# One cosine table folded out of the sine's turns, and small vector work given to GpSimd, in a fused state-space and feed-forward kernel

## The chip, the cores and the metric

The kernel runs on one core of a Trainium2 chip. The core has five engines that each work through their own list of instructions in the written order: TensorE (PE in the profile; its weight loads are PEld), VectorE (DVE), ScalarE (ACT), GpSimd (POOL) and SyncE (SP), which here only issues transfers. An engine that waits for another holds up everything written behind that instruction on its own list. The metric is device microseconds of one execution; the kernel's time is the median over several executions.

## The reference

Two branches read the same normalized input and are added to it. x has 2048 rows (time steps) of 512 features in bfloat16; P = 512 states, F = 1376.

```python
xn = layernorm(x)
# branch A: a diagonal complex state-space model
Lam, Bmat, Cmat = Lambda_re + 1j*Lambda_im, B_re + 1j*B_im, C_re + 1j*C_im
Lam_bar = exp(exp(log_dt) * Lam)
B_bar = ((Lam_bar - 1) / Lam)[:, None] * Bmat
Bu = einsum("bld,pd->blp", xn, B_bar)
for t in range(L):                      # 2048 steps, P complex states
    h = Lam_bar * h + Bu[:, t]
y = 2 * real(einsum("blp,dp->bld", h, Cmat)) + xn * Dskip
# branch B: a gated feed-forward net
f = (silu(xn @ w_gate) * (xn @ w_up)) @ w_down
out = x + y + f
```

## The kernel before, in words

**Tiling.** The 2048 rows are cut into four chunks of 512, and each chunk into four tiles of 128 rows. Tensors are held with features or states on the 128 partitions: 512 features or states are four blocks (NQ = 4), and F = 1376 is ten blocks of 128 and a rest of 96. One matmul takes a 128x128 weight block against 512 columns. All matmul results go to PSUM, which is held as eight banks of 128x512 in float32 (`bank()`); a bank is used again only when the engine that reads its old contents is through.

**What a chunk goes through.** Normalization (`ln_stats` L204, `ln_rstd` L212, `ln_nb` L216; chunks 2 and 3 are normalized on ScalarE by `norm_act` L233 to L236, which needs `nb`), and a transposing transfer on SyncE's queue (`xT_dma`). The projection to the states (`bproj_tile`, matmuls L380, eight groups of four for the real and imaginary part of four blocks; ScalarE copies each bank out at L382). The gate and up products (`gu_mm`, L500; ScalarE evicts gate through Silu at L519 and up at L520; VectorE multiplies the two at L515). The remaining 96 columns of F go through `gateup_last` and `up_pair` (copies to `ul` on ScalarE at L548). The down product (L795 in `out_ffn`, L771 in `out_pair`).

**The complex recurrence made real.** The rotating part of the state is taken off before the recurrence and put back behind it. Tables of cosine and sine of j times the angle (`c16`, `s16`, 128 x 4 x 512 in bfloat16) multiply the projected input; then VectorE runs a real first-order scan per block and part with the modulus `r_t` (L466, eight scans a chunk), and the result is rotated back. A rotation has two forms. `rotation` (L384) does six passes of 128x2048 on VectorE. `rotation_dma` (L414) does four: two `side` products (L423 or L425), two `main` products (L428), and the additions are made by accumulating transfers that GpSimd issues (`join`, L431). It needs the negated sine for one of its sides: `neg_s16`, which `negate_table` (L409) makes on ScalarE in the space of two tiles, `part_end` and `jidx`. Between two chunks the last state is turned by the angle of 512 steps: `carry` (L470 to L482), six operations on 128x4 numbers; the scans of the next chunk start from it.

**The tables** (`table_ops`, L297). For each half of the blocks: `turns` (two products of the index j by the angle in turns), `half` for the sine and again for the cosine (add a quarter turn for the cosine, round by adding a large constant, L314, subtract both, L315), and the two sine activations (L319). Their scratch tiles are named `pm`, of which there are three.

**The coefficients** (`params_b`, L337): sixteen operations on 128x4 numbers that give `c2re`, `nc2re` and `nc2im`, among them a reciprocal. `c_ops` (L354) uses them to fold the input factor into C: ScalarE scales a block of C (L363, tile `cm`), VectorE combines it with the other part (L366, tile `CF`), eight times.

**Outputs.** For chunk 3 the states' output product is eight matmuls a tile (`out_ssm`, L807). For chunks 0, 1 and 2 it is a two-by-two block scheme with seven products in place of eight (`out_ssm_seven`, L670, matmuls L690). Its sums of states and of weights are made by ScalarE and by accumulating transfers (`state_sums`, `weight_sums`), and its results are put together by VectorE (`add`, L702) from PSUM banks and scratch (`six`, `seven`, `one`, `five`, and `finish`, L711, for the four result tiles `res`).

**What sets the order.** The program is written in the order of TensorE's work. VectorE's queue work and the work that goes with it is kept in a list, `backlog`, of operations with a cost in microseconds each (`queue`, L829). After each group of matmuls the program calls `pump` (L845) with the time that the group takes on TensorE. That time is added to `owed`, and operations are taken from the list and written out as long as `owed` is at least half the cost of the first one; each takes its cost off `owed` (`step`, L836). Products and the adds of `out_ssm_seven` also take their cost off. `need(tag)` writes out everything up to the last operation of a tag. `step` also writes out the ScalarE part of the next operations ahead of time (`AHEAD`, for the scalings of L363). So a cost figure decides nothing on the chip, but it decides where in each engine's list an operation stands. The list in question begins with the tables and the normalization of chunk 1 (L954 to L960), goes on with the coefficients and the rotation of chunk 0 (L1073) mixed with the normalization of chunks 2 and 3 (L1075 to L1078), then chunk 1, the folding of C (L1105), chunk 2 (L1115), and chunk 3 (L1131 to L1134).

Of the kernel before, what the change touches and what calls it, by code (L numbers as in the profile page):

```python
# [23 lines left out]
def kernel(  # L24
# [143 lines left out]
    jidx = const.tile([128, CW], F32, name="jidx")  # L168
    nc.gpsimd.iota(out=jidx[:], pattern=[[1, CW]], base=0, channel_multiplier=0, allow_small_or_imprecise_dtypes=True)
# [6 lines left out]
    part_end = const.tile([128, D], F32, name="part_end")  # L176
# [119 lines left out]

    def table_ops():  # L297

        ops = []
        for q0 in range(0, NQ, 2):  # L300
            box = {}

            def turns(q0=q0, box=box):
                box["tt"] = ssm.tile([128, 2, CW], F32, name="pm", bufs=3)
                for qq in range(2):
                    V.tensor_scalar(out=box["tt"][:, qq, :], in0=jidx[:], scalar1=ws2[:, 0, q0 + qq:q0 + qq + 1],
                                    scalar2=None, op0=ALU.mult)

            def half(dst, shift, q0=q0, box=box):
                tt = flat(box["tt"][:])  # L310
                if shift:
                    V.tensor_scalar(out=tt, in0=tt, scalar1=shift, scalar2=None, op0=ALU.add)
                km = box[shift] = ssm.tile([128, 2, CW], F32, name="pm", bufs=3)
# [4 lines left out]
            def sine(dst, shift, q0=q0, box=box):  # L318
                nc.scalar.activation(out=flat(dst[:, q0:q0 + 2, :]), in_=flat(box[shift][:]), func=ACT.Sin,  # L319
                                     scale=-TWO_PI_LO)  # L320

            ops += [(0.9, turns), (1.8, lambda half=half: half(s16, 0.0)),
                    (1.2, lambda half=half: half(c16, 0.25)), (0.6, lambda sine=sine: sine(s16, 0.0)),
                    (0.6, lambda sine=sine: sine(c16, 0.25))]
# [12 lines left out]
    def params_b():  # L337
        tt(t_a[:], lre, lre, ALU.mult)
        tt(t_b[:], lim, lim, ALU.mult)
        tt(den[:], t_a[:], t_b[:], ALU.add)  # L340
        V.reciprocal(out=den[:], in_=den[:])
        tt(lbi[:], r_t[:], sin1[:, 0, :], ALU.mult)
        tt(lbr[:], r_t[:], cos1[:, 0, :], ALU.mult)
        V.tensor_scalar(out=lbr[:], in0=lbr[:], scalar1=-1.0, scalar2=None, op0=ALU.add)
        tt(t_a[:], lbr[:], lre, ALU.mult)
        tt(t_b[:], lbi[:], lim, ALU.mult)
        tt(num_re[:], t_a[:], t_b[:], ALU.add)
        tt(t_a[:], lbi[:], lre, ALU.mult)
        tt(t_b[:], lbr[:], lim, ALU.mult)
        tt(num_im[:], t_a[:], t_b[:], ALU.subtract)  # L350
        for dst, num, s in ((c2re, num_re, 2.0), (nc2re, num_re, -2.0), (nc2im, num_im, -2.0)):
            V.scalar_tensor_tensor(out=dst[:], in0=num[:], scalar=s, in1=den[:], op0=ALU.mult, op1=ALU.mult)
# [54 lines left out]
    neg_s16 = [t[:].bitcast(BF16).rearrange("p (q j) -> p q j", q=2) for t in (part_end, jidx)]  # L407

    def negate_table():  # L409
        for q in range(NQ):  # L410
            yield 1, lambda q=q: nc.scalar.activation(out=neg_s16[q // 2][:, q % 2], in_=s16[:, q], func=ACT.Copy,
                                                      scale=-1.0)

    def rotation_dma(src, dst, back):  # L414
# [3 lines left out]
        def side(i):  # L418
            t = box[i] = ssm.tile([128, NQ, CW], BF16, name="pm", bufs=3)
            if i == (1 if back else 0):  # L420
                for h, table in enumerate(neg_s16):
                    q = slice(2 * h, 2 * h + 2)
                    V.tensor_tensor(out=t[:, q], in0=src()[:, i, q], in1=table, op=ALU.mult)  # L423
            else:
                V.tensor_tensor(out=t[:], in0=src()[:, i], in1=s16[:], op=ALU.mult)  # L425
# [742 lines left out]
```

## Time and profile before

| what | value |
|---|---|
| median of three runs (lowest to highest) | 176.67 us (176.61 to 177.15) |
| the profiled execution | 176.73 us, its span 174.9 us |
| granted TensorE clock, mean | 1.00 |
| TensorE busy | 171.3 us, 98% of the span |
| VectorE busy | 160.2 us, 92% |
| ScalarE busy | 102.6 us, 59% |
| GpSimd busy | 55.1 us, 32% |

The span is the time from the first to the last instruction that the profiler recorded; the execution's own time is 1.8 us longer. In the rows below a line of a timeline has the start, the length, the engine, the line of the kernel, the operation, the tiles it writes and reads, and how many instructions in a row it stands for; square brackets give the idle time before it and what ended it. A line of a group has the count, the busy time, the mean of one in nanoseconds and the idle time before.

### The profile page before, as it was taken

The page shows a single profiled execution, that of the slowest core. Times are in us where ns is not written, and L with a number is a line of the kernel's source. Part 1 is how long each engine was busy: PE and PEld are TensorE (multiplying, and loading weights), DVE is VectorE, ACT ScalarE, POOL GpSimd, SP SyncE. Part 2 cuts the span into 40 slices and gives each one's busy share as a digit, 9 for nine tenths or more (in the row PEclk, how much of TensorE's full clock was granted, in tenths as well). Part 3 has the DMA queues.
Part 4 walks back from the last instruction along what each step waited for, and adds up shares of the span by engine and source line. Part 5 has one row for each costly group of instructions (what it writes and reads, how often), then busy time and mean ns, then how long its engine had stood idle before and what let it go on. Part 6 is the DMA issues. An engine that isn't in the chain of part 4 may idle for free.

```text
span 174.9 us, 2876 instructions
## 1 busy us (share of the span) xinstructions
PE 171.3 (98%) x1026; PEld 90.3 (52%) x1026; DVE 160.2 (92%) x255; ACT 102.6 (59%) x194; POOL 55.1 (32%) x57
## 2 busy tenths in 40 slices
PE   8999999999999999999999999999999999999993
PEld 3877544444444444444444584468444444447743
DVE  3879998999999999899999989997999999995884
ACT  4587898969599889999767760001297632001100
POOL 7050120000300163403555052550473402518440
PEclk9999999999999999999999999999999999999999
DMA  5998499996239079996999988592199999687954
GB/s 161 301 196 198 91 255 91 322 282 139 46 61 287 0 150 168 205 182 175 124 117 128 198 145 100 69 141 43 24 172 207 198 152 237 82 95 78 181 146 139
DMA packets 45758, 26.61 MB, mean 152 GB/s; under 512 B 22272, under 2 KB 44544, under 8 KB 45728
## 3 DMA queue, kind: packets, MB, share of 16 engines
q0 software_dynamic: 12624, 11.67, 47.2%
q1 hardware_dynamic: 30672, 13.61, 34.2%
q10 hardware_dynamic: 2448, 1.15, 2.9%
q8 instruction: 8, 0.13, 0.3%
q14 instruction: 6, 0.05, 0.1%
HBM read 8.33 MB, written 4.19 MB: 72 GB/s over the span
## 4 chain that ended last, share of the span: by engine, by line
PE 96%; DMA 1%; DVE 1%; ACT 0%; issue 0%
PE ps L500 36%; PE ps L380 16%; PE ps L690 11%; PE ps L795 10%; PE ps L771 10%; PE ps L807 4%; PE ps L896 2%; PE ps L553 2%; PE ps L977 2%; PE ps L598 2%; DMA xall<-in_A_x_dram 1%; PE ps L545 1%; PE ps L245 1%; DVE stats L205 0%; ACT gu_last L226 0%; DVE xall L222 0%
## 5 line engine op out<-in xcount | busy, mean ns | idle before, releaser
L500 PE MATMUL ps<-xnT,wu 128*128 128x512 bf16 (+1 forms) x148 | 36.6, 373 | 0.0
L500 PE MATMUL ps<-xnT,wg 128*128 128x512 bf16 (+1 forms) x148 | 36.6, 373 | 0.0
L466 DVE TENSOR_TENSOR_SCAN g<-r_t,car,u 128x512 bf16<-128x512 f32 x24 | 28.8, 1263 | 0.0
L380 PE MATMUL ps<-xnT,BT 128*128 128x512 bf16 x128 | 28.3, 379 | 0.0
L519 ACT ACTIVATE guT<-ps 128x512 bf16<-128x512 f32 (+1 forms) x40 | 24.0, 601 | 5.8 <-PE ps L500 2.8
L520 ACT CAST u_all<-ps 128x512 bf16<-128x512 f32 (+1 forms) x40 | 23.4, 584 | 4.1 <-PE ps L500 4.0
L500 PEld LDWEIGHTS <-wu 128*128 128x128 bf16 x148 | 14.5, 98 | 16.6
L500 PEld LDWEIGHTS <-wg 128*128 128x128 bf16 x148 | 14.4, 98 | 16.5
L382 ACT CAST u<-ps 128x512 bf16<-128x512 f32 x32 | 18.3, 587 | 5.2 <-PE ps L380 5.0
L380 PEld LDWEIGHTS <-BT 128*128 128x128 bf16 x128 | 12.3, 98 | 15.2 <-issue 1.0
L723 ACT COPY guT<-ps 128x512 f32<-128x512 f32 x2 | 1.2, 586 | 28.5 <-PE ps L690 28.5
L795 PE MATMUL ps<-wd_sb,guT 128*128 128x512 bf16 x80 | 17.6, 379 | 0.0
L771 PE MATMUL ps<-wd_sb,guT 128*128 128x512 bf16 x80 | 17.4, 379 | 0.0
L214 POOL TENSOR_TENSOR rstd<-ve,neg_half 128x2 f32<-128x2 f32 (+1 forms) x4 | 5.6, 1390 | 29.9 <-DVE ve L213 29.9
L515 DVE TENSOR_TENSOR guT<-guT,u_all 128x1024 bf16<-128x1024 bf16 x20 | 13.3, 678 | 0.0
L795 PEld LDWEIGHTS <-guT 128*128 128x128 bf16 x80 | 7.7, 98 | 9.6 <-issue 0.4
L771 PEld LDWEIGHTS <-guT 128*128 128x128 bf16 x80 | 7.8, 98 | 9.4
L431 POOL DMA_DIRECT2D wt<-pm x4 | 3.6, 909 | 25.9 <-DVE wt L428 16.7
L205 DVE BATCH_NORM_STATS2 stats<-xall 128x6 f32<-128x512 bf16 x14 | 9.5, 679 | 2.1 <-DMA xall<-in_A_x_dram 2.1
L466 DVE TENSOR_TENSOR_SCAN g<-r_t,u 128x512 bf16<-128x512 f32 x8 | 9.3, 1205 | 0.0
L617 POOL DMA_DIRECT2D xnT<-wt x3 | 3.9, 1290 | 14.0 <-DMA CT<-CF 8.4
L719 POOL DMA_DIRECT2D out_dram<-res x8 | 8.0, 1836 | 0.0
(176 smaller groups left out, 283.9 us busy)
## 6 DMA issues: line engine op xcount, KB each, us to landing
wt<-pm POOLq DMA_DIRECT2D x4, 512.0 KB, 5.0
u<-pm POOLq DMA_DIRECT2D x4, 512.0 KB, 5.9
wd_sb<-in_B_w_down_dram SPq DMA_DIRECT2D x2, 640.0 KB, 8.4
xall<-in_A_x_dram SPq DMA_DIRECT2D x1, 1024.0 KB, 6.5
out_dram<-res POOLq DMA_DIRECT2D x8, 128.0 KB, 5.7
out_dram<-xall POOLq DMA_DIRECT2D x2, 512.0 KB, 8.9
xnT<-wt POOLq DMA_DIRECT2D x3, 256.0 KB, 4.8
xnT<-wt SPq DMA_DIRECT2D x3, 256.0 KB, 7.5
```

What stands on the lines that cost most here:

```text
L205: nc.vector.bn_stats(out=stats[:, n, :], in_=xall[:, n, :])
L380: nc.tensor.matmul(ps[:], lhsT=BT[:, part, k, q * 128:(q + 1) * 128], rhs=xnT[:, k, c * CW:(c + 1) * CW], start=(k == 0), stop=(k == KD - 1))
L382: nc.scalar.copy(out=u_tiles[c][:, part, q, :], in_=ps[:])
L466: V.tensor_tensor_scan(out=g()[:, part, q, :], data0=r_t[:, q:q + 1].to_broadcast([128, CW]), data1=u_tiles[c][:, part, q, :], initial=ini ...
L500: nc.tensor.matmul(ps[:fs, lo:hi], lhsT=wslice(groups, fi, k), rhs=xnT[:, k, c * CW + lo:c * CW + hi], start=(k == 0), stop=(k == KD - 1))
L515: products.append(lambda: V.tensor_tensor(out=g, in0=g, in1=u, op=ALU.mult))
L519: nc.scalar.activation(out=gu_tile(c)[:, fi, 0:hi], in_=psg[:, 0:hi], func=ACT.Silu)
L520: nc.scalar.copy(out=u_tile(c, fi)[:, fi % 2, 0:hi], in_=psu[:, 0:hi])
L690: nc.tensor.matmul(place(i), lhsT=a[:, q, i * 128:(i + 1) * 128], rhs=b[:, q, :], start=(start and q == 0), stop=(stop and q == NQ - 1))
L719: nc.gpsimd.dma_start(out=out_v[:, n, :], in_=res[:], accum_op=ALU.add)
L771: nc.tensor.matmul(o[:], lhsT=gu_tiles[k][:, fi, i * 128:(i + 1) * 128], rhs=wd_sb[:, fi, :], start=(fi == 0), stop=False)
L795: nc.tensor.matmul(o[:], lhsT=gu_tiles[c][:, fi, i * 128:(i + 1) * 128], rhs=wd_sb[:, fi, lo:hi], start=(fi == 0), stop=False)
```

## The change

The cosine table is no longer rounded for itself. `fold` takes the sine's turns, which lie between minus a half and a half, and clears their sign bit (one pass, `bitwise_and` with 0x7fffffff on the bits). The cosine is then the sine of a quarter turn minus that: the second activation has the bias `quarter`, a constant of half of pi that GpSimd writes once. The shift by a quarter turn, the rounding and the subtraction of the cosine go.

`part_end` and `jidx` become two halves of one tile, `ends`, and `neg_s16` is one table over both, so that each negated side is one product and not two.

`params_b` is written for GpSimd, seventeen operations there; only the reciprocal stays on VectorE. The factors of 2 and -2 are now put into `den` between the last products. The six operations of each `carry` are made by GpSimd.

Three cost figures are changed with this: the cosine's rounding at 1.2 becomes `fold` at 0.6, `params_b` goes from 1.5 to 0.1, and `carry` from 0.8 to 0.0. The list and the calls of `pump` stay as they were. VectorE's list therefore lacks what is taken off it and holds the rest of the same work, in places in another order, as the planner writes it out; ScalarE's, GpSimd's and SyncE's lists are in places in another order too. TensorE's list is the same in the same order.

```diff
-    jidx = const.tile([128, CW], F32, name="jidx")
-    nc.gpsimd.iota(out=jidx[:], pattern=[[1, CW]], base=0, channel_multiplier=0, ...)
+    ends = const.tile([128, 2, CW], F32, name="ends")
+    part_end, jidx = ends[:, 0, :], ends[:, 1, :]
+    nc.gpsimd.iota(out=jidx, pattern=[[1, CW]], base=0, channel_multiplier=0, ...)
...
-    part_end = const.tile([128, D], F32, name="part_end")
...
+    quarter = sm("quarter", 1)
+    nc.gpsimd.memset(quarter[:], PI_LO / 2)
...
-            def half(dst, shift, q0=q0, box=box):
+            def half(q0=q0, box=box):
                 tt = flat(box["tt"][:])
-                if shift:
-                    V.tensor_scalar(out=tt, in0=tt, scalar1=shift, scalar2=None, op0=ALU.add)
-                km = box[shift] = ssm.tile([128, 2, CW], F32, name="pm", bufs=3)
+                km = box["s"] = ssm.tile([128, 2, CW], F32, name="pm", bufs=3)
                 V.tensor_scalar(out=flat(km[:]), in0=tt, scalar1=MAGIC, scalar2=None, op0=ALU.add)
                 V.scalar_tensor_tensor(out=flat(km[:]), in0=flat(km[:]), scalar=MAGIC, in1=tt,
                                        op0=ALU.subtract, op1=ALU.subtract)
...
+            def fold(box=box):
+                km = box["c"] = ssm.tile([128, 2, CW], F32, name="pm", bufs=3)
+                bits = [flat(t[:]).bitcast(mybir.dt.uint32) for t in (km, box["s"])]
+                V.tensor_scalar(out=bits[0], in0=bits[1], scalar1=0x7fffffff, scalar2=None, op0=ALU.bitwise_and)
+
+            def sine(dst, turn, bias, q0=q0, box=box):
+                nc.scalar.activation(out=flat(dst[:, q0:q0 + 2, :]), in_=flat(box[turn][:]), func=ACT.Sin,
+                                     scale=-TWO_PI_LO, bias=bias)
...
-            ops += [(0.9, turns), (1.8, lambda half=half: half(s16, 0.0)),
-                    (1.2, lambda half=half: half(c16, 0.25)), (0.6, lambda sine=sine: sine(s16, 0.0)),
-                    (0.6, lambda sine=sine: sine(c16, 0.25))]
+            ops += [(0.9, turns), (1.8, half), (0.6, fold), (0.6, lambda sine=sine: sine(s16, "s", 0.0)),
+                    (0.6, lambda sine=sine: sine(c16, "c", quarter[:]))]
...
     def params_b():
-        tt(t_a[:], lre, lre, ALU.mult)
...
-        for dst, num, s in ((c2re, num_re, 2.0), (nc2re, num_re, -2.0), (nc2im, num_im, -2.0)):
-            V.scalar_tensor_tensor(out=dst[:], in0=num[:], scalar=s, in1=den[:], op0=ALU.mult, op1=ALU.mult)
+        G = nc.gpsimd
+
+        def gg(o, a, b, op):
+            G.tensor_tensor(out=o, in0=a, in1=b, op=op)
+
+        gg(t_a[:], lre, lre, ALU.mult)
...
+        G.tensor_scalar(out=den[:], in0=den[:], scalar1=2.0, scalar2=None, op0=ALU.mult)
+        gg(c2re[:], num_re[:], den[:], ALU.mult)
+        G.tensor_scalar(out=den[:], in0=den[:], scalar1=-1.0, scalar2=None, op0=ALU.mult)
+        gg(nc2re[:], num_re[:], den[:], ALU.mult)
+        gg(nc2im[:], num_im[:], den[:], ALU.mult)
...
-    neg_s16 = [t[:].bitcast(BF16).rearrange("p (q j) -> p q j", q=2) for t in (part_end, jidx)]
+    neg_s16 = ends[:].rearrange("p a j -> p (a j)").bitcast(BF16).rearrange("p (q j) -> p q j", q=NQ)
...
         def side(i):
             t = box[i] = ssm.tile([128, NQ, CW], BF16, name="pm", bufs=3)
-            if i == (1 if back else 0):
-                for h, table in enumerate(neg_s16):
-                    q = slice(2 * h, 2 * h + 2)
-                    V.tensor_tensor(out=t[:, q], in0=src()[:, i, q], in1=table, op=ALU.mult)
-            else:
-                V.tensor_tensor(out=t[:], in0=src()[:, i], in1=s16[:], op=ALU.mult)
+            V.tensor_tensor(out=t[:], in0=src()[:, i], in1=neg_s16 if i == back else s16[:], op=ALU.mult)
...
-                V.tensor_tensor(out=t[:, 0, :], in0=gre, in1=c5, op=ALU.mult)
...
+                nc.gpsimd.tensor_tensor(out=t[:, 0, :], in0=gre, in1=c5, op=ALU.mult)
...
-            ops.append((0.8, carry))
+            ops.append((0.0, carry))
...
-    queue("ssm0", [(1.5, params_b)] + fwd0[0:6])
+    queue("ssm0", [(0.1, params_b)] + fwd0[0:6])
```

44 lines of the change are left out of this document (20 added, 24 removed).

## The prediction

> **What bounds the kernel now.** I read the page's busy times first, then the chain that ended last, then the single timelines of TensorE, VectorE, ScalarE and GpSimd. From the page, and under it three pieces of the chain in order of time (start, length, what):
>
> ```profile
> span 174.9 us, 2876 instructions
> PE 171.3 (98%) x1026; PEld 90.3 (52%) x1026; DVE 160.2 (92%) x255; ACT 102.6 (59%) x194; POOL 55.1 (32%) x57
> 99.50 6.11 PE ps L690 x56
> ...
> 122.95 17.27 PE ps L500 x80
> ...
> 158.89 6.36 PE ps L690 x56
> ```
>
> TensorE is the bound, and it has no gaps: 80 matmuls in 17.27 us are 0.216 us each, and every such piece comes to the same 0.216. The only loose time I find after the head is in the products of L690: the same 56 take 6.11 us at one place and 6.36 at another. So 0.25 us is about all that a better fed TensorE could win. The change moves no matmul. Its question is whether TensorE still gets its PSUM banks in time: there are eight, and each next matmul group waits until the engine that reads the old contents is through.
>
> VectorE is 92% busy and works in the written order, with the order set by the kernel's cost figures. The change alters those figures, so it moves VectorE's work against TensorE's. That is where I looked longest.
>
> **Part 1, the cosine table.** VectorE's groups, and the start and end of the coefficients (columns: line, operation, count, busy us, mean ns; and start, length):
>
> ```profile
> L315 DVE SCALAR_TENSOR_TENSOR pm<-pm 128x1024 f32<-128x1024 f32 x4 | 4.9, 1226 | 0.1
> L314 DVE TENSOR_SCALAR pm<-pm 128x1024 f32<-128x1024 f32 x4 | 2.8, 692 | 0.6 <-DVE pm L312 0.5
> 29.59 0.15 DVE L331 TENSOR_TENSOR t_a<-prm 128x4 f32<-128x4 f32 x1
> 31.62 1.22 DVE L390 TENSOR_TENSOR pm<-u,c 128x2048 bf16<-128x2048 bf16 x1
> 27.90 1.06 ACT L319 ACTIVATE s<-pm 128x1024 bf16<-128x1024 f32 x1
> 29.81 1.08 ACT L319 ACTIVATE c<-pm 128x1024 bf16<-128x1024 f32 x1
> ```
>
> Each of the two cosine halves loses a shift and a rounding (0.69 each) and a subtraction (1.23), and gets one mask. The mask has no row. Its bounds are nothing and the 1.23 of a two-input pass; I take 0.69, the one-input pass of the same shape. That frees 3.8 us. The coefficients free 31.62 - 29.59 = 2.0 us less the reciprocal that stays, so VectorE could start rotating chunk 0 near 26. It cannot, because the rotation needs the whole cosine table, and the second sine activations stand on ScalarE behind a gate tile of fixed time. The sine starts at 27.90 as now; the cosine now follows it directly, and ends at 27.90 + 1.06 + 1.08 = 30.0. So of 5.6 us freed, 1.6 arrive. ScalarE's gate tile slips by one activation, with the banks of four tiles as cover.
>
> **Part 2, coefficients, reciprocal, folded tables, one negated table.** Seventeen small GpSimd operations take the place of fifteen VectorE ones. One of the kind stands on GpSimd now:
>
> ```profile
> 10.39 0.20 POOL L280 TENSOR_TENSOR dre<-dt_t,prm 128x4 f32<-128x4 f32 x1
> ```
>
> The results are needed only by ScalarE's scalings (L363, from 67.54 in the next rows), so I cost them at nothing; without that cover they would cost 17 x 0.20 = 3.4 us. The negated table in one piece makes one pass of 1.2 us out of two halves of 0.69 each, four times: 0.1 us each. The merged tile and the constant are free.
>
> **Part 3, the order up to 76 us.** These rows carry the next steps (four timelines, VectorE, GpSimd, ScalarE, TensorE):
>
> ```profile
> 58.92 1.19 DVE L428 TENSOR_TENSOR wt<-g,c 128x2048 bf16<-128x2048 bf16 x1
> 60.63 0.16 DVE L213 TENSOR_SCALAR ve<-mv 128x4 f32<-128x4 f32 x1
> 60.70 0.68 DVE L515 TENSOR_TENSOR guT<-guT,u_all 128x1024 bf16<-128x1024 bf16 x1
> 63.57 0.16 DVE L217 SCALAR_TENSOR_TENSOR nb<-mv,rstd 128x4 f32<-128x4 f32 x1 [0.30 <-POOL rstd L214]
> ...
> 117.93 0.13 DVE L475 TENSOR_TENSOR ct<-g,cos 128x4 f32<-128x4 bf16 x1
> ...
> 118.70 0.69 DVE L702 TENSOR_TENSOR guT<-ps,guT 128x512 f32<-128x512 f32 x1 [0.15 <-PE ps L690]
> 60.42 0.97 POOL L431 DMA_DIRECT2D wt<-pm  x1 [15.11 <-DVE wt L428]
> 61.12 0.87 POOL L1113 DMA_DIRECT2D dsk_bc<-in_A_Dskip_dram  x1
> 61.72 1.81 POOL L214 TENSOR_TENSOR rstd<-ve,neg_half 128x4 f32<-128x4 f32 x1
> 57.76 1.19 ACT L548 CAST ul<-ps 64x512 bf16<-64x512 f32 x2 [0.32 <-PE ps L545]
> 63.77 1.52 ACT L235 ACTIVATE xn_end<-xall,nb,rstd 128x512 bf16<-128x512 bf16 x2
> 67.54 0.72 ACT L363 ACTIVATE cm<-CT,c2re 128x512 f32<-128x512 bf16 x1
> 73.92 0.70 ACT L363 ACTIVATE cm<-CT,nc2re 128x512 f32<-128x512 bf16 x1
> 22.15 1.06 ACT L382 CAST u<-ps 128x512 bf16<-128x512 f32 x2
> 57.66 7.08 PE L380 MATMUL ps<-xnT,BT 128*128 128x512 bf16 x32
> ```
>
> From the rotation (31.62) to the variance step `ve` of the last chunk (60.63) VectorE has 29.0 us of work. In the changed order that stretch lacks a carry (118.70 - 117.93 less the wait of 0.15, 0.6) and two products (0.68 each, 0.6 with the overlap). So `ve` comes at 30.0 + 27.2 = 57.2. GpSimd has first the join of the state (0.3 behind the L428 pass, 0.7 until its next), then rstd (1.81); then `nb` of 0.16: 57.2 + 0.3 + 0.7 + 1.8 + 0.2 = 60.2, where it was 63.73.
>
> But the cost figures have also moved the four normalizations of the last chunk forward on ScalarE. They stood behind six of the eight copies of chunk 2's projections; now they stand before all eight and before the two `ul` copies. ScalarE comes to them before 57.76, where the `ul` copies start now, and waits two to three microseconds for `nb`. Queued behind are the `ul` copies, which hold a bank that the eighth projection group needs. That group starts at 57.66 + 28 x 0.216 = 63.71. Four normalizations (twice 1.52) and the two copies (1.2) from 60.2 end at 64.4, so TensorE loses 0.7 us here.
>
> The same ScalarE queue then sets VectorE's next step. From the first normalization to the eighth scaling are 73.92 - 63.77 = 10.15 us; now two `ul` copies (1.2) and six projection copies (0.48 each, half of the 22.15 row less its overlap) are in it too, 4.1 us. The eighth scaling starts at 60.2 + 10.15 + 4.1 = 74.45, 0.5 later than before. VectorE waits for each of them:
>
> ```profile
> 72.22 3.40 DVE L366 SCALAR_TENSOR_TENSOR CF<-CT,nc2im,cm 128x512 bf16<-128x512 bf16 x5 [0.50 <-ACT cm L363]
> 75.54 9.51 DVE L466 TENSOR_TENSOR_SCAN g<-r_t,car,u 128x512 bf16<-128x512 f32 x8
> ```
>
> So the scans of chunk 1 start at 76.05 and not at 75.54. The whole saving on VectorE so far is lost in these waits.
>
> **Part 4, the sums of the early outputs, where the time goes.** VectorE must add up the seven products of chunk 1 (L702), and TensorE's next gate and up groups (L500) take the banks that these adds free. VectorE and TensorE there now, beside the first add at 118.70 above:
>
> ```profile
> 104.17 0.69 DVE L702 TENSOR_TENSOR u_all<-u_all,cm 128x512 f32<-128x512 f32 x1 [0.47 <-ACT cm L608]
> 120.12 0.69 DVE L702 TENSOR_TENSOR guT<-guT 128x512 f32<-128x512 f32 x1 [0.73 <-ACT guT L726]
> 120.73 1.22 DVE L425 TENSOR_TENSOR pm<-g,s 128x2048 bf16<-128x2048 bf16 x1
> 121.87 0.68 DVE L702 TENSOR_TENSOR guT<-ps,guT 128x512 f32<-128x512 f32 x1
> 122.59 0.69 DVE L702 TENSOR_TENSOR guT<-guT 128x512 f32<-128x512 f32 x1
> 122.79 1.03 PE L500 MATMUL ps<-xnT,wg 128*128 128x512 bf16 x4
> 124.51 1.03 PE L500 MATMUL ps<-xnT,wg 128*128 128x512 bf16 x4
> 126.24 1.03 PE L500 MATMUL ps<-xnT,wg 128*128 128x512 bf16 x4
> ```
>
> Now the first add starts at 118.70, as soon as TensorE allows it. With carries and folds costed at nothing or little, the planner hands VectorE its queue sooner in the written order. In the changed order five rotation passes (two sides, two mains of chunk 2, one side of chunk 3), 1.14 us each, stand before that add instead of behind it, and one main and one side stand between the later adds. From 75.54 to 118.70 are 43.2 us; without the idle 0.5, a carry (0.6) and the stretch from 117.93 with the other (0.8) they are 41.3. With 5.7 more from 76.05 the first add starts at 123.05. It ends 0.7 later, at 123.75; TensorE wants the bank at 122.79. The second add (behind a second add of its pair and a main): 123.05 + 0.72 + 0.6 + 1.14 = 125.5, ends 126.2, wanted at 124.51. The first of the four last adds: 125.5 + 0.72 + 0.6 + 1.14 = 127.95, ends 128.65, wanted at 126.24. The three banks after it come every 0.6 us, faster than TensorE's 0.86. So TensorE leaves this place 128.65 - 126.24 = 2.4 us late, which includes the 0.7 of part 3, since the wants are absolute times. Behind it ScalarE's next tile, which also waits for these adds, has a bank or more of cover, and VectorE has free time before the end; TensorE has none to give back.
>
> **Carries, stores, SyncE.** The carries of chunks 0 and 1 have 10 us and more before the scans that read them. On GpSimd's queue the second is put between accumulating transfers of the sums, which wait for each other anyway. On SyncE the last chunk's transposes now go ahead of the copy of x to the output; the copy is needed by the stores of results long after, and the sums' copies stay behind both. I take nothing, with up to 1 us if a transfer is late.
>
> **The sum.** The profiled execution took 176.73, its span 174.9 and 1.8 around it; the median of the runs is 176.67. 176.7 + 2.4 = 179.1.
>
> **Rivals.** *Later still.* The third carry stands on GpSimd ahead of the join of chunk 2, which must land before VectorE reuses its buffer, at 126.8 by the steps above. Its six operations cost between the 0.20 of L280 and the 1.81 of rstd each:
>
> ```profile
> 163.92 2.12 POOL L709 TENSOR_TENSOR guT<-guT,xall 128x1024 f32<-128x1024 f32 x1 [2.87 <-DVE guT L702]
> 164.47 2.12 DVE L702 TENSOR_TENSOR guT<-guT 128x512 f32<-128x512 f32 x1
> wt<-pm POOLq DMA_DIRECT2D x4, 512.0 KB, 5.0
> ```
>
> I take 0.4, nearest to the 0.20 of the same operation, more because VectorE is busy: the scans of chunk 2 end near 117.6, the carry at 120.3, the join has landed (5.0) at 125.4: no cost. From 0.65 each it decides; at 1.0 the carry ends at 123.9, the join lands at 128.9, and the time is 179.1 + 2.1 = 181.2. The two instructions at 164 speak for it: a VectorE add of 0.69 took 2.12 beside a GpSimd one. The Trainium skill (SBUF — State Buffer, section SBUF: two separate sides) says that VectorE with two SBUF inputs and GpSimd lock each other out of a shared port for a whole instruction; the two rows agree. By that rule alone each small operation waits out up to one pass of 1.22, and this rival is the outcome.
>
> *Only ScalarE's wait.* VectorE is 2 us ahead of my count and its adds are in time: +0.7, 177.4. Against it: ScalarE's late scalings.
>
> *Not slower.* VectorE keeps more of what is taken off it: `nb` is ready before 59.5, so ScalarE is not late, and VectorE comes to the adds 2.4 us sooner than I count, so that each ends before its bank is wanted. 176.7, at best 176.4 with the 0.25 of L690. For it speaks that VectorE's total falls by 7 us; against it the fixed 30.0 of the cosine table. That the change does not free VectorE at all would give the forecast or worse.
>
> **How the numbers follow.** Forecast 0.62, later still 0.18, only ScalarE 0.08, no change 0.09, faster 0.03. The forecast's own range is 178.1 to 180.2 (1 us of VectorE's clock either way moves it one for one); with the rivals 177.3 to 181.2. About 0.3% is what a measurement here can tell from no change: faster 0.03, within 0.09, slower 0.88.
>
> **What would show it.** VectorE idle before the chunk-0 rotation until about 30.0; ScalarE idle some 3 us before the first `xn_end`; a TensorE gap of under 1 us near 63.7 and gaps near 123 to 129 with L702 adds as releasers; five rotation passes before the first add. A TensorE without gaps, adds that begin by 121, or carries of over 0.65 us an operation would make the forecast wrong.

## The result, and the profile after

The changed kernel takes 182.87 us (median of four runs, 182.72 to 182.98), where the kernel before takes 176.64 (median of four): a ratio of 1.035, with a 95% interval of 1.032 to 1.037. It is slower by 6.2 us; the prediction was 179.1 with a range up to 181.2. The profiled execution took 182.72 with a span of 180.9. From here on lines of the changed kernel are meant where it is spoken of: L507 is the gate and up matmul (L500 before), L697 the products of the early outputs (L690), L709 their adds (L702), L555 the `ul` copies (L548), L473 the scans, L432, L435 and L438 the sides, mains and joins, L482 to L487 the carry.

From the page, and under it the waits of TensorE behind the start that have a releaser in the profile (total us, times, longest us):

```profile
PE 171.9 (95%) x1026; PEld 89.7 (50%) x1026; DVE 152.8 (84%) x214; ACT 101.9 (56%) x194; POOL 71.6 (40%) x93
```

```profile
PE ps L697 <- DMA CT<-CT: 4.2, 2, 2.5
PE ps L507 <- DVE res L709: 0.6, 1, 0.6
PE ps L393 <- ACT ul L555: 0.6, 1, 0.6
```

TensorE is as busy as before (171.9 against 171.3), and VectorE has 7.4 us less to do. The 6 us are waits of TensorE, in three places: against the kernel before it falls 0.4 us back at L393, 4.8 more at L697 (4.2 of it shows as idle time) and 0.75 more at L507. Where a wait ends is seen in its timeline (start, length, count, and in brackets the idle time before):

```profile
64.13 1.02 PE L393 MATMUL ps<-xnT,BT 128*128 128x512 bf16 x4 [0.56 <-ACT ul L555]
104.21 3.05 PE L697 MATMUL ps<-CT,xnT 128*128 128x256 bf16 x24 [2.55 <-DMA CT<-CT]
108.95 1.03 PE L697 MATMUL ps<-CT,wt 128*128 128x256 bf16 x8 [1.69 <-DMA CT<-CT]
132.23 1.02 PE L507 MATMUL ps<-xnT,wg 128*128 128x512 bf16 x4 [0.59 <-DVE res L709]
```

A naive reading adds these up and blames the second place most: TensorE comes out of it at 108.95, where the same product began at 103.70 before, 5.25 us later. The last row is the one to hold on to. The same four matmuls started at 126.24 before: TensorE leaves this place 6.0 us late, and there is no wait behind it. What sets the time is whatever holds that row, and VectorE's timeline shows it:

```profile
29.74 1.23 DVE L403 TENSOR_TENSOR pm<-u,c 128x2048 bf16<-128x2048 bf16 x1 [3.71 <-ACT c L325]
77.21 2.46 DVE L473 TENSOR_TENSOR_SCAN g<-r_t,car,u 128x512 bf16<-128x512 f32 x2 [1.16 <-DMA u<-pm]
80.04 7.16 DVE L473 TENSOR_TENSOR_SCAN g<-r_t,car,u 128x512 bf16<-128x512 f32 x6 [0.37 <-DMA u<-pm]
124.55 0.68 DVE L709 TENSOR_TENSOR guT<-ps,guT 128x512 f32<-128x512 f32 x1
130.36 1.23 DVE L432 TENSOR_TENSOR pm<-u,s 128x2048 bf16<-128x2048 bf16 x1 [1.84 <-DMA wt<-pm]
131.50 2.47 DVE L709 TENSOR_TENSOR res<-ps,guT 128x512 bf16<-128x512 f32 x4
```

From 80 us to 128.5 VectorE has no idle time above 0.2 us in this trace, so the TensorE waits at 101 to 107 did not delay it. It comes to the first add of chunk 1 at 124.55 (118.70 before), then waits 1.84 us for a join, and starts the four last adds at 131.50. The first of them frees the bank for the row at 132.23.

The two DMA names in these rows lead to GpSimd's queue. Its timeline at the carries of chunks 1 and 2, and under it VectorE's passes at the same time as the first of them:

```profile
92.04 1.61 POOL L482 TENSOR_TENSOR ct<-g,cos 128x4 f32<-128x4 bf16 x1
92.35 1.91 POOL L483 TENSOR_TENSOR ct<-g,sin 128x4 f32<-128x4 bf16 x1
92.50 2.90 POOL L484 TENSOR_TENSOR ct<-g,sin 128x4 f32<-128x4 bf16 x1
93.63 2.90 POOL L485 TENSOR_TENSOR ct<-g,cos 128x4 f32<-128x4 bf16 x1
94.33 3.33 POOL L486 TENSOR_TENSOR car<-ct 128x4 f32<-128x4 f32 x1
96.61 1.66 POOL L487 TENSOR_TENSOR car<-ct 128x4 f32<-128x4 f32 x1
97.62 1.90 POOL L624 DMA_DIRECT2D CT<-CT  x1
...
119.56 5.12 POOL L482 TENSOR_TENSOR ct<-g,cos 128x4 f32<-128x4 bf16 x1
124.64 0.19 POOL L483 TENSOR_TENSOR ct<-g,sin 128x4 f32<-128x4 bf16 x1
125.69 1.77 POOL L438 DMA_DIRECT2D wt<-pm  x2 [0.27 <-PE ps L697]
```

```profile
93.54 0.68 DVE L522 TENSOR_TENSOR guT<-guT,u_all 128x1024 bf16<-128x1024 bf16 x1
94.14 1.21 DVE L417 TENSOR_TENSOR wt<-pm 128x2048 bf16<-128x2048 bf16 x1
95.28 1.21 DVE L403 TENSOR_TENSOR pm<-u,c 128x2048 bf16<-128x2048 bf16 x1
96.41 1.21 DVE L403 TENSOR_TENSOR pm<-u,s 128x2048 bf16<-128x2048 bf16 x1
97.55 0.68 DVE L522 TENSOR_TENSOR guT<-guT,u_all 128x1024 bf16<-128x1024 bf16 x1
98.15 1.21 DVE L403 TENSOR_TENSOR pm<-u,s 128x2048 bf16<-128x2048 bf16 x1
```

Add start and length of the six operations: they end at 93.65, 94.26, 95.40, 96.53, 97.66 and 98.27. VectorE begins a new pass at 93.54, 94.14, 95.28, 96.41, 97.55 and 98.15. Each small GpSimd operation ends 0.11 to 0.12 us behind a border between two VectorE passes, one per border: 6.2 us for work that takes 6 x 0.15 elsewhere. The transfers behind it in the queue, first CT<-CT, leave that much later; the queue was 2.7 us behind already (the transfer ahead of the carry leaves at 91.27, before at 88.53). The second carry is worse placed: its first operation ends at 124.68, 0.13 behind the start of the first VectorE pass that reads PSUM (124.55), and the next five follow at 0.15 each. The join behind it leaves at 125.69, and VectorE waits for it at 130.36.

### The profile page after: what moved, and what is told of

It is laid out like the page before. It is cut to its first block, busy times and chain, and to the rows that moved or that the text cites. A ratio compares the mean times of both kernels' runs of the same rounds, so it can differ in the third digit from the quotient of the medians.

```text
span 180.9 us, 2875 instructions
## 1 busy us (share of the span) xinstructions
PE 171.9 (95%) x1026; PEld 89.7 (50%) x1026; DVE 152.8 (84%) x214; ACT 101.9 (56%) x194; POOL 71.6 (40%) x93
## 4 chain that ended last, share of the span: by engine, by line
PE 41%; DVE 23%; DMA 19%; ACT 5%; POOL 5%; SPq 3%; issue 3%; POOLq 0%; DVEq 0%
PE ps L507 12%; PE ps L778 10%; DMA xnT<-wt 8%; DVE g L473 8%; PE ps L697 4%; PE ps L814 4%; PE ps L393 4%; DMA xnT<-xnT 4%; DMA CT<-CT 4%; DVE stats L205 3%; DVE pm L403 3%; DMA wt<-pm 3%; PE ps L903 2%; PE ps L880 2%; DVE pm L432 2%
## 5 line engine op out<-in xcount | busy, mean ns | idle before, releaser
L507 PE MATMUL ps<-xnT,wg 128*128 128x512 bf16 (+1 forms) x148 | 36.7, 373 | 0.6 <-DVE res L709 0.6
L507 PE MATMUL ps<-xnT,wu 128*128 128x512 bf16 (+1 forms) x148 | 36.6, 373 | 0.0
L473 DVE TENSOR_TENSOR_SCAN g<-r_t,car,u 128x512 bf16<-128x512 f32 x24 | 29.2, 1264 | 1.5 <-DMA u<-pm 1.5
L393 PE MATMUL ps<-xnT,BT 128*128 128x512 bf16 x128 | 28.5, 379 | 0.6 <-ACT ul L555 0.6
L507 PEld LDWEIGHTS <-wg 128*128 128x128 bf16 x148 | 14.4, 98 | 17.4 <-issue 0.9
L507 PEld LDWEIGHTS <-wu 128*128 128x128 bf16 x148 | 14.5, 98 | 16.6
L393 PEld LDWEIGHTS <-BT 128*128 128x128 bf16 x128 | 12.3, 98 | 15.9 <-issue 1.7
L395 ACT CAST u<-ps 128x512 bf16<-128x512 f32 x32 | 17.8, 596 | 4.0 <-PE ps L393 3.9
L802 PE MATMUL ps<-wd_sb,guT 128*128 128x512 bf16 x80 | 17.6, 379 | 0.0
L802 PEld LDWEIGHTS <-guT 128*128 128x128 bf16 x80 | 7.7, 98 | 9.6 <-issue 0.4
L624 POOL DMA_DIRECT2D xnT<-wt x3 | 4.4, 1473 | 12.9 <-DMA CT<-CF 10.0
L482 POOL TENSOR_TENSOR ct<-g,cos 128x4 f32<-128x4 bf16 x3 | 6.9, 2309 | 6.0 <-DVE g L473 6.0
L473 DVE TENSOR_TENSOR_SCAN g<-r_t,u 128x512 bf16<-128x512 f32 x8 | 9.2, 1206 | 0.0
L697 PEld LDWEIGHTS <-wt 128*128 128x128 bf16 x72 | 6.9, 98 | 3.7 <-issue 2.7
```

Of the source, the lines that this page charges most:

```text
L393: nc.tensor.matmul(ps[:], lhsT=BT[:, part, k, q * 128:(q + 1) * 128], rhs=xnT[:, k, c * CW:(c + 1) * CW], start=(k == 0), stop=(k == KD - 1))
L395: nc.scalar.copy(out=u_tiles[c][:, part, q, :], in_=ps[:])
L473: V.tensor_tensor_scan(out=g()[:, part, q, :], data0=r_t[:, q:q + 1].to_broadcast([128, CW]), data1=u_tiles[c][:, part, q, :], initial=ini ...
L507: nc.tensor.matmul(ps[:fs, lo:hi], lhsT=wslice(groups, fi, k), rhs=xnT[:, k, c * CW + lo:c * CW + hi], start=(k == 0), stop=(k == KD - 1))
L697: nc.tensor.matmul(place(i), lhsT=a[:, q, i * 128:(i + 1) * 128], rhs=b[:, q, :], start=(start and q == 0), stop=(stop and q == NQ - 1))
L802: nc.tensor.matmul(o[:], lhsT=gu_tiles[c][:, fi, i * 128:(i + 1) * 128], rhs=wd_sb[:, fi, lo:hi], start=(fi == 0), stop=False)
```

## The experiments

All runs are compared with runs of the kernel before on the same chip (176.4 to 176.7). Theory from here on: the order that the planner's lower figures give makes VectorE late at the adds of chunk 1, and this alone would cost nearly all; GpSimd's slow carries make a second loss that the first hides, and add a little through the join. The rival that the waits suggest: the GpSimd carries are the loss.

**Carries back on VectorE.** In the changed kernel:

```diff
-                nc.gpsimd.tensor_tensor(out=t[:, 0, :], in0=gre, in1=c5, op=ALU.mult)
+                V.tensor_tensor(out=t[:, 0, :], in0=gre, in1=c5, op=ALU.mult)
...
```

> The changed kernel with the three carries made by VectorE again, in the places where they stand now, at the cost figure 0.0. Theory (two delays, one hidden behind the other): GpSimd's slow carry of chunk 1 makes TensorE wait 4.8 us for the sums of weights at 101 to 107 us, but behind it VectorE's adds of chunk 1 are late anyway, because of the order. So the waits at 101 to 107 go, and the one at L507 grows: the first res add started at 131.50 after a wait of 1.84 for a join, without it at 129.7, plus two carries of 0.5 each, so TensorE goes on at 131.4 and not at 126.24: 5.2 us lost in all, 181.3 to 181.9 us. Rival (the carries on GpSimd are the whole loss but the 0.7 at 63 us): 177.4 us.

Measured: 182.47 us, ratio 1.034 (1.032 to 1.036). TensorE's waits for VectorE, and VectorE at the adds:

```profile
PE ps L507 <- DVE guT L709: 2.2, 2, 1.6
PE ps L802 <- DVE u_all L709: 1.4, 1, 1.4
PE ps L507 <- DVE res L709: 0.6, 1, 0.6
```

```profile
126.24 0.69 DVE L709 TENSOR_TENSOR guT<-ps,guT 128x512 f32<-128x512 f32 x1
131.24 2.48 DVE L709 TENSOR_TENSOR res<-ps,guT 128x512 bf16<-128x512 f32 x4
```

The waits for CT<-CT are gone from the list, every one of them, and the time fell by 0.4 us. In their place TensorE waits for adds, at L802 (chunk 0, not expected) and at L507, and the res adds start at 131.24 instead of 131.50. The rival of 177.4 falls. The theory's 181.3 to 181.9 was 0.6 too low, since the three carries put VectorE back by 1.7 us and not 1.0: the first add moved from 124.55 to 126.24.

**The carry of chunk 1 alone back on VectorE** (the engine is chosen by chunk, `V if c == 1 else nc.gpsimd`):

> The changed kernel with the carry of chunk 1 alone made by VectorE again. Theory (the wait of 4.8 us at 101 to 107 us is hidden by a later one): that wait goes, and TensorE is held instead at L507 by the res adds, which come 0.5 us later than in the changed kernel, since VectorE has the carry to do and the join behind the carry of chunk 2 is as late as before: 182.7 to 183.5 us, no gain. Rival (the waits add up): 178.0 to 178.5.

Measured: 182.93 us, ratio 1.036 (1.035 to 1.038). The waits at 101 to 107, 4.8 us of delay, are gone and nothing is gained, as expected: TensorE waits for VectorE's adds instead, at the last of them for 2.3 us and then leaves that place at 132.54 (132.23 in the changed kernel). The waits do not add up.

```profile
PE ps L508 <- DVE res L710: 2.3, 1, 2.3
```

**The carry of chunk 2 alone back on VectorE** (`V if c == 2 else nc.gpsimd`):

> The changed kernel with the carry of chunk 2 alone made by VectorE again; those of chunks 0 and 1 stay on GpSimd. Theory: the join wt<-pm of chunk 2 no longer waits behind GpSimd's carry, VectorE loses its 1.84 us wait for it, and the first res add comes at about 130.2, before TensorE, held 5.5 us by the earlier waits, wants that bank at 131.8. So the 0.75 us at L507 goes and the rest stays: 182.0 to 182.3 us. Rival (VectorE's lateness there is the order alone): 182.7 to 183.3 us.

Measured: 182.44 us, 182.05 to 183.14, ratio 1.033 (1.030 to 1.036), between the two expectations. The waits at L507 are gone, and the res adds start at 130.13, before TensorE wants them (one line added moves L709 to L710):

```profile
130.13 2.48 DVE L710 TENSOR_TENSOR res<-ps,guT 128x512 bf16<-128x512 f32 x4
```

What holds TensorE in this kernel are the transfers behind carry 1: it waits 2.2 us for CT<-CT and 0.7 for a copy behind an early product, and its clock is halved from about 107.6 to 111.0 (last section). The two losses are nearly equal, so removing either shows the other. The times do not part the two expectations, which differ by 0.4 us; the row above and the missing waits do.

**The cost figures alone, in the kernel before:**

```diff
-            ops.append((0.8, carry))
+            ops.append((0.0, carry))
...
-                    (1.2, lambda half=half: half(c16, 0.25)), ...
+                    (0.6, lambda half=half: half(c16, 0.25)), ...
...
-    queue("ssm0", [(1.5, params_b)] + fwd0[0:6])
+    queue("ssm0", [(0.1, params_b)] + fwd0[0:6])
```

> The kernel before with the three cost figures of the change alone (0.6, 0.1, 0.0); every operation is as before. Theory (the order by itself makes VectorE's adds late): the last chunk's variances come at 59.4, nb at 62.4, the ul copies end at 66.6 and TensorE loses 2.9 us there; the scans of chunk 1 start 2.8 us later than now, the first add of chunk 1 at 126.5, its first res add ends about 132.4, where TensorE wants 126.24: 6 us lost in all, 181.5 to 183.5 us. Rival (figures without the moved operations do little): 176.7 to 177.4.

Measured: 183.90 us, ratio 1.042 (1.040 to 1.044), 0.4 above the range given. The first add of chunk 1, at 118.70 in the kernel before, expected at 126.5:

```profile
127.79 0.69 DVE L702 TENSOR_TENSOR guT<-ps,guT 128x512 f32<-128x512 f32 x1
```

The sum behind the range was off in two terms: the wait for the `ul` copies was 1.4 us and not 2.9, and ahead of the scans of chunk 1 VectorE waited 1.19 and 0.38 us for the joins, which the sum did not have. No operation is other than before, on any engine. Three numbers in the planner's list cost 7.5 us (176.4 in the runs beside it), more than the whole change does, because VectorE here has the work that the change takes off it.

**The cost figures of before, in the changed kernel**, once with the carries on GpSimd and once with the carries on VectorE:

```diff
-            ops.append((0.0, carry))
+            ops.append((0.8, carry))
...
-            ops += [(0.9, turns), (1.8, half), (0.6, fold), ...
+            ops += [(0.9, turns), (1.8, half), (1.2, fold), ...
...
-    queue("ssm0", [(0.1, params_b)] + fwd0[0:6])
+    queue("ssm0", [(1.5, params_b)] + fwd0[0:6])
```

> The changed kernel with the three cost figures of before (1.2 for the fold, 1.5 for the coefficients, 0.8 for a carry); all the new operations stay, carries on GpSimd. VectorE's order is that of before again. Theory: no wait at 63 us, and the adds of chunk 1 in time; what is left is the carry of chunk 1 on GpSimd, which now stands behind the first accumulation CT<-CT and ahead of the second: it begins at about 91.5 (where that transfer is issued), takes six passes of VectorE, 6 us, and the last CT<-CT is issued at 101.3 instead of 95.30 and lands at 106, where TensorE wants it at 103.7: 2.3 us lost at L697, 178.5 to 179.5 us. Rival A (the engine of the carries does not matter, the order is everything): 176.7. Rival B (the carries alone are the loss): 181.5 or more.

> The changed kernel with carries on VectorE and the three cost figures of before: what is left of the change is the folded cosine table, the single negated table and the coefficients on GpSimd. VectorE's, ScalarE's and SyncE's order is that of before. Theory: TensorE has no gap to give back, so 176.4 to 176.8 us although VectorE has some 6 us less to do; 176.4 if the 0.14 us at L697 near 162 goes too. Rival (the coefficients on GpSimd or the cosine behind the sine cost something of their own): 177.2 or more.

With the carries on VectorE: 176.50 us, ratio 1.000 (0.998 to 1.001), and TensorE's waits list has nothing behind the start:

```profile
PE ps L880 <- PEq L1159: 0.8, 1, 0.8
```

So the folded cosine, the single negated table and the coefficients on GpSimd cost nothing and bring nothing. With the carries on GpSimd the four runs took 178.98, 181.46, 182.81 and 183.95, a median of 182.13. The 178.98 is the run at full TensorE clock and lies in the range of the theory; the others had a mean clock of 0.98 to 0.99, and in the one with a profile (183.95) the clock was halved for some 7 us behind a wait of 3.6 us at L697, for which the profile has no releaser. That profile also shows something late that the theory does not have, the joins ahead of the scans of chunk 1:

```profile
u<-pm POOLq DMA_DIRECT2D x2, 512.0 KB, 10.2
78.07 2.46 DVE L473 TENSOR_TENSOR_SCAN g<-r_t,car,u 128x512 bf16<-128x512 f32 x2 [2.39 <-DMA u<-pm]
```

With the carries on VectorE the joins left at the same times (68.77 and 70.00, here 68.72 and 69.95), landed in 6.5 us, and the scans began without a wait at 75.33. Why they were slow here is open; the copy of x had left at 54.16, long before. GpSimd's queue was 4.2 us behind before it came to the carry (first CT<-CT at 95.50, there at 91.29), and the carry then took 5.8 us. So this execution cannot price the carry. Rival A falls by the times: all four runs lie 2.1 us and more above the slowest of ten runs (176.31 to 176.91) of the kernel that differs only in the engine of the carries. How much of that is the carry and how much the late transfers stays open. Rival B is not excluded by these times; it falls by the kernel with all carries on VectorE, which takes 182.47 without any.

**The carries on GpSimd alone, in the kernel before** (cost figure 0.8 kept):

```diff
-                V.tensor_tensor(out=t[:, 0, :], in0=gre, in1=c5, op=ALU.mult)
+                nc.gpsimd.tensor_tensor(out=t[:, 0, :], in0=gre, in1=c5, op=ALU.mult)
...
```

> The kernel before with one thing changed: the six operations of each carry are written for GpSimd; the cost figure stays 0.8, so VectorE's order is that of before without the carries. Theory: each of the six operations of chunk 1's carry takes as long as one two-input pass of VectorE, about 1 us; they stand between two accumulating transfers, the last CT<-CT is issued about 6 us later and lands about 2 us after TensorE wants it at L690 near 103.7: 178.3 to 179.5 us. The carry of chunk 2 costs nothing there, since a sum from PSUM follows the scans. Rival (small operations cost their own 0.2 us): 176.4 to 176.8.

Measured: ten runs from 176.33 to 179.74 us, median 177.79, at a granted clock of 0.999 or 1.000; without the two longest the ratio is 1.005 (1.001 to 1.009). Five runs lie below the range expected, four in it and one above. GpSimd in a run without a wait at L690:

```profile
91.57 1.20 POOL L475 TENSOR_TENSOR ct<-g,cos 128x4 f32<-128x4 bf16 x1
95.75 0.65 POOL L480 TENSOR_TENSOR car<-ct 128x4 f32<-128x4 f32 x1
96.34 1.29 POOL L617 DMA_DIRECT2D CT<-CF  x1
97.13 1.81 POOL L617 DMA_DIRECT2D CT<-CT  x1
```

The carry takes 4.8 us, and CT<-CF leaves at 96.34 where it left at 91.54, as the theory has it. But the last CT<-CT is issued right behind it, at 97.13 and not at 101: I had taken it to wait for the transfer ahead to land. So it leaves 1.8 us later than before (95.30), and in this run TensorE does not wait for it. The mechanism is there, and its price in this run was 2 us too high. That the longer runs, up to 3.4 us over the shortest, lost their time at this place is likely but not shown: they have no trace.

**The carry of chunk 1 written twice, in the changed kernel:**

```diff
+                for _ in range(2 if c == 1 else 1):
+                    nc.gpsimd.tensor_tensor(out=t[:, 0, :], in0=gre, in1=c5, op=ALU.mult)
...
```

> The changed kernel with the six operations of chunk 1's carry written twice on GpSimd, one set behind the other (the second gives the same numbers). Theory (each small GpSimd operation waits for the end of a VectorE pass, about 1 us each): the transfers of the weights' sums behind it are issued 5 to 6 us later still, CT<-CT lands at about 110 and not at 104; TensorE's waits at L697 grow by as much and the later one at L507 goes: 182.87 + 5.5 - 0.75 = 187.6, between 186.5 and 188.5 us. Rival (small operations cost their own 0.2 us each, and the delay of the transfers has another cause): 183 to 184 us.

Measured: 184.79 us, 183.92 to 186.16, ratio 1.045 (1.041 to 1.048). The twelve operations take from 92.32 to 103.42:

```profile
92.32 1.73 POOL L483 TENSOR_TENSOR ct<-g,cos 128x4 f32<-128x4 bf16 x1
...
101.76 1.66 POOL L488 TENSOR_TENSOR car<-ct 128x4 f32<-128x4 f32 x1
102.26 2.41 POOL L625 DMA_DIRECT2D CT<-CT  x1
```

CT<-CT is issued 4.6 us later than in the changed kernel (97.62), 0.8 us for each operation added, four times its own length; the rival's 0.2 falls by this, though one of the runs lies in the rival's range. TensorE restarts at 107.88, 3.7 later. The execution with this profile is the slowest of the four, 3.4 over the changed kernel: TensorE comes out of the products 4.2 us later, less the 0.75 of the wait at L507 that they now cover. The median is only 1.9 over it, and the shortest run only 1.1. So the mechanism is shown by the trace and the forecast of the time was too high: it had 5.5 to 6 us for the six operations, which cost 4.6, and it let the second wait for CT<-CT (1.69) stand, which the longer first one swallows. Against that it did not have the halved clock behind the wait, some 2.5 us at the products (last section).

**The account charged at one place.** In the kernel with carries on VectorE, one line is added:

```diff
+    owed[0] -= 4.8
     bproj_chunk(3)
```

> The changed kernel with carries on VectorE and one line more: 4.8 us are taken off the planner's account ahead of the projections of chunk 3, so that from there on VectorE's order is nearly that of before (no rotation pass of chunks 2 and 3 ahead of the first adds of chunk 1); the early part, with the normalizations ahead of the ul copies, stays. Theory (two places: ul copies 1.2, then the adds behind five rotation passes): the adds are in time, only the 1.2 us at 63 us is left, 177.5 to 178.0 us, against 182.47 without the line. Rival (VectorE is late for a reason other than the order of the passes): 181 or more.

Measured: 177.88 us, ratio 1.008 (1.005 to 1.010), where the same kernel without the line took 182.47. TensorE's only wait behind the start is the one for the `ul` copies:

```profile
PE ps L393 <- ACT ul L555: 1.0, 1, 1.0
```

This is the theory's strongest support: the same operations on the same engines, only put out later by the planner, give back 4.6 us. The joins ahead of the scans are late here too (they land in 10.3 us, and VectorE waits 0.86 and 0.36), and it costs nothing: with the order repaired VectorE has room for it.

**The copy of x to the output issued earlier**, ahead of the gate and up products of chunk 1, also with carries on VectorE:

```diff
+    nc.sync.dma_start(out=out[0, 0:(NT - 2 * TPC) * 128, :], in_=A_x[0, 0:(NT - 2 * TPC) * 128, :])
     gateup_chunk(1)
-    nc.sync.dma_start(out=out[0, 0:(NT - 2 * TPC) * 128, :], in_=A_x[0, 0:(NT - 2 * TPC) * 128, :])
```

> The changed kernel with carries on VectorE, and the 1 MB copy of x to the output issued on SyncE ahead of the gate and up products of chunk 1, so that it does not wait behind the transposes of the last chunk. Theory (the late copy slows the joins u<-pm, for which the scans of chunk 1 wait 1.6 us): the joins land in some 6 us and not 10, that wait goes, every later step of VectorE comes 1.5 us sooner, and TensorE with it: 180.7 to 181.3 us against 182.47. Rival (the joins are slowed by the copies of the states' sums, not by this copy): 182.3 to 182.6.

Measured: 180.75 us, ratio 1.024 (1.023 to 1.026), 1.7 us less than 182.47. The joins in the changed kernel and here, and VectorE at the scans and at the adds:

```profile
u<-pm POOLq DMA_DIRECT2D x2, 512.0 KB, 10.6
u<-pm POOLq DMA_DIRECT2D x2, 512.0 KB, 6.5
```

```profile
76.77 8.33 DVE L473 TENSOR_TENSOR_SCAN g<-r_t,car,u 128x512 bf16<-128x512 f32 x7
129.71 2.48 DVE L709 TENSOR_TENSOR res<-ps,guT 128x512 bf16<-128x512 f32 x4
```

The joins land in 6.5 us (10.6 in the changed kernel, 6.3 in the kernel before), the wait ahead of the scans is gone, and the res adds start 1.5 us sooner. In the changed kernel that copy of 1 MB stood behind the transposes of the last chunk and left SyncE at 67.27, together with the joins; before, it left at 54.58.

None of these kernels is faster than the one before. With TensorE at 98% of the span there was nothing to win by taking work from VectorE.

## Why the prediction was wrong

**Right.** The direction, the place, and the steps up to 76 us. Predicted and measured: chunk 0 rotates from 30.0 (29.74), held by the cosine's activation; `ve` of the last chunk at 57.2 (57.05); `nb` done at 60.2 (60.04); the `ul` copies done at 64.4 (64.08); TensorE's loss there 0.7 (0.56 of idle in the row at 64.13, 0.4 later than the 63.71 of the forecast). The mask took 0.69 as chosen. The coefficients on GpSimd at nothing, and the negated table at nothing for TensorE, are borne out by the kernel that keeps only these at 176.50. And the cause: that five rotation passes ahead of the first add would make TensorE wait for the banks at L507 is what the planner runs show, from both sides (183.90 for the figures alone, 177.88 when they are charged back).

**Wrong: the size of part 4.** It had TensorE leave the adds 2.4 us late, at 128.65. It left at 132.23, 6.0 late. The first add came 1.5 us later than its 123.05, and from there to the last adds it took 6.95 us and not 4.9. Behind these are two terms that were set to nothing and were not:

- "I take nothing, with up to 1 us if a transfer is late", of SyncE's order. The scans of chunk 1 were to start at 76.05. VectorE was ready at 76.06 (the CF row starts at 72.66 and lasts 3.40 in the trace), but the joins u<-pm came 1.5 us later (1.16 and 0.37 of idle in the rows at 77.21 and 80.04). The run with the early copy shows the term: 1.5 us at the adds, 1.7 us in the time. It counts only in this order; in the kernel with the account charged, the joins were as late and nothing was lost.
- "I take 0.4, nearest to the 0.20 of the same operation" for a small GpSimd operation, and with it "no cost" for the third carry. The rival *later still* had said from which price on it decides, 0.65, and this is what happened: 1.04 each for carry 1, and 5.12 for the first operation of carry 2. Of the 5.12, 1.9 went by while GpSimd was still issuing stores (until 121.45), which the prediction's sum also left out. The join was issued at 125.69 and VectorE stood 1.84 us. With carry 2 on VectorE the res adds start at 130.13 and not at 131.50.

The prediction's rival at 181.2, and 1.5 for the late joins on top, make 182.7: the measured 182.87. That it comes out so closely is partly luck: the rival had six operations of 1.0, and the trace has one of 5.12 and five at 0.15. The mistake in the choice is plain in hindsight. The row taken for the price (0.20 at 10.39) stood beside no rotation pass, and the operations to be priced stood amid nothing else. The row at 164 with 2.12 was the nearest in kind of neighbour, if not in kind of operation. The rule quoted there from the Trainium skill (SBUF — State Buffer, section SBUF: two separate sides) agrees with this trace as far as carry 1 goes: each operation ends just behind a border of VectorE's passes. For a transfer issued by GpSimd beside a VectorE copy the Trainium skill (SBUF — State Buffer, section A bandwidth-pool intuition that's wrong (but worth ruling out)) states a release about 115 ns behind the end of the VectorE instruction. Here the small operations end 0.11 to 0.12 us behind the start of the next pass, which is only 0.04 to 0.05 behind the recorded end of the last one, so that figure is not confirmed for them.

**Not foreseen: 4.8 us that did not matter.** "On GpSimd's queue the second is put between accumulating transfers of the sums, which wait for each other anyway" was wrong. Six operations of 1.04 delayed the transfers, and TensorE stood for them at 101 to 107. It cost nothing only because VectorE would have held TensorE at 132 all the same. With carry 2 on VectorE that hold is gone, and this becomes the loss (182.44, from the waits for CT<-CT and for one copy and the clock that fell behind them).

## What to carry to other kernels

In a list whose order comes out of cost figures, lowering a figure moves everything behind it; what has to be checked is not the operation that got cheaper but the first consumer of a bank further on. Two waits of the bound engine do not add up as long as the engine that it waits for last is not itself delayed by the earlier wait: the later one swallows those ahead of it, so a wait is worth its price only at the last place where the engine is held, and taking away the larger wait may show nothing. A small operation on GpSimd is to be priced by the VectorE passes that run beside it, and by the transfers that stand behind it in the same queue.

## What the runs showed that I had not expected

**One border, one operation, mostly.** The price of a GpSimd operation on 128x4 numbers went from 0.15 to 1.04 us with what VectorE ran beside it: 0.15 apart beside a pass that reads PSUM (from 124.64), one per border beside passes with two inputs from SBUF (from 92). Why the first operation of carry 2 let four such borders pass, at 120.0 to 123.4, the runs do not tell; GpSimd issued four stores until 121.45, which explains the first two at most. It is no single case: with the cost figures put back and the carries on GpSimd, the fifth operation of carry 1 took 2.64 us, from 99.33 to 101.97, across the borders at 99.57 and near 100.7.

**A wait can halve TensorE's clock.** In the kernel with carry 1 written twice, TensorE stood 5.94 us for CT<-CT. The products behind it, and the granted clock by stretches of time (stretch, its length, busy time and count of TensorE, weight loads, VectorE, ScalarE, GpSimd, then the clock, DMA share and GB/s):

```profile
107.88 5.28 PE L698 MATMUL ps<-CT,xnT 128*128 128x256 bf16 x24 [5.94 <-DMA CT<-CT]
```

```profile
103.00:105.00 2.00, 0.00 (x0) 0.00 (x0) 2.00 (x4) 0.00 (x0) 2.00 (x3) 1.00 0.07 14
109.00:111.00 2.00, 2.00 (x11) 1.37 (x10) 1.26 (x2) 0.00 (x0) 2.00 (x3) 0.50 0.84 96
```

The clock falls to 0.50 toward the end of the wait and stays there until about 113.4: the same 24 products take 5.28 us where they took 2.78 in the kernel before. The same happened behind the wait of 3.58 us in the profiled run of the kernel with the cost figures put back and the carries on GpSimd. In the changed kernel's profiled run the two waits of 2.55 and 1.69 left it at 1.00; two of its other runs have a mean clock of 0.991 and no trace. The Trainium skill (TensorE: Matmul & The Clock Gate, section Part 1: The HAM clock gate) states the return to half speed after an idle window of about 3.4 us. The four waits named so far lie on either side of it, but the kernel with carry 2 on VectorE does not fit: there waits of 0.72 and 2.23 us with 1.03 us of products between them were enough.

```profile
107.42 1.73 PE L698 MATMUL ps<-CT,wt 128*128 128x256 bf16 x8 [2.23 <-DMA CT<-CT]
107.00:109.00 2.00, 1.58 (x9) 1.13 (x9) 2.00 (x2) 0.00 (x0) 0.00 (x0) 0.65 1.24 140
```

Eight such products take 1.04 us at full clock. So the length of a single wait does not decide by itself, and the runs here do not give a shortest wait that is safe.
